# One attention and gate kernel: decay folded into V, token-block loads, row-tiled head pairs, one pipeline

## The chip, the core and the metric

The kernel runs on one core of a Trainium2 chip. Its time is the device time of one launch in microseconds (us), taken as the median of 3 runs. The core has TensorE (PE, with its weight loads PEld), VectorE (DVE), ScalarE (ACT), GpSimd (POOL) and SyncE (SP), which here issues most DMAs. Each engine runs its own instruction list in order and waits on semaphores for the others.

## The reference

Inputs are q, k, v of 8 batches, 8 heads, 576 positions, 64 numbers each, a selection signal s of 8 x 8 x 576, and three weights. In the reference's terms:

```
cum    = cumsum(max(s, 0))                       # per head, over positions
scores = q @ k.T / 8 + min(-(cum_q - cum_k), 0)  # causal: later keys are masked
attn   = softmax(scores) ;  x = attn @ v         # heads side by side: x is 576 x 512
gate   = sigmoid(sum over 5 taps of conv_w[t] * x shifted by 4 - t)
out    = (gate * (x @ w_val)) @ w_out            # 8 x 576 x 512, float32
```

The decay is a difference of running sums, so exp(-(cum_q - cum_k)) is a factor of the query times a factor of the key, and the query's factor cancels when a row is divided by its sum.

## The kernel before, in words

The tokens of a batch are cut in key blocks of 128, 128, 128, 128 and 64 (`kbs`, `kbo`). A set-up part computes the running sums with TensorE (`cumT`, lines 72 to 86) and loads the weights.

**Attention**, one batch after another (line 114 on): blocks of q, k and v come in as float32; TensorE transposes q and k in float32, two heads at a time (line 135), and ScalarE and VectorE copy each head to `QT` and `KT` (lines 142, 144). Row 64 of these holds the query's running sum and ones, so that a score matmul with 65 rows adds the query's decay (line 159); the key's decay is the bias of the exp (line 162). VectorE multiplies each diagonal block by a triangle (166). The products with V (line 175) carry a column of ones for the row sums; VectorE and ScalarE divide (180 to 184), TensorE transposes the result (187), and a copy puts it in `xT`.

**Gate**, after the last batch, for four groups of channels and eight batches (line 196 on): ScalarE multiplies by each tap (202, 206), VectorE adds (209), ScalarE takes the sigmoid (210), TensorE computes x @ w_val (214), VectorE multiplies (217). **Output**, last: TensorE (226), a copy on ScalarE (229), a store (230).

What runs when is set twice: the lists that the engines run come out of a scheduler that interleaves the program's operations by its own estimate of when they are ready, and the tile pools set how many copies of a tile exist (`ps_s`, `ps_t`, `ps_a`: two PSUM tiles each). All loads of q, k, v and all stores are issued by SyncE; the small loads of `cwT` (line 99) and of the decay rows (119) by ScalarE.

Of the kernel before, what the change touches and what calls it, by code (L numbers as in the profile page):

```python
# [8 lines left out]
FP32 = mybir.dt.float32  # L9
BF16 = mybir.dt.bfloat16  # L10
AF = mybir.ActivationFunctionType
ALU = mybir.AluOpType


@with_exitstack
def kernel(
# [11 lines left out]
    nc = tc.nc  # L28
    B, H, S, D = 8, 8, 576, 64
    DM = 512  # L30
    NKB = 5
    kbs = [128, 128, 128, 128, 64]
    kbo = [0, 128, 256, 384, 512]
    NT = B * S

    const_p = ctx.enter_context(tc.tile_pool(name="const", bufs=1))
    cum_p = ctx.enter_context(tc.tile_pool(name="cum", bufs=1))
    qk_in_p = ctx.enter_context(tc.tile_pool(name="qkin", bufs=3))
    qkt_p = ctx.enter_context(tc.tile_pool(name="qkt", bufs=2))
    v_p = ctx.enter_context(tc.tile_pool(name="v", bufs=2))  # L40
    attn_p = ctx.enter_context(tc.tile_pool(name="attn", bufs=2))
    x_p = ctx.enter_context(tc.tile_pool(name="x", bufs=1))
    moe_p = ctx.enter_context(tc.tile_pool(name="moe", bufs=1))
    glu_p = ctx.enter_context(tc.tile_pool(name="glu", bufs=1))
    gate_p = ctx.enter_context(tc.tile_pool(name="gate", bufs=2))
    oout_p = ctx.enter_context(tc.tile_pool(name="oout", bufs=3))
    ps_s = ctx.enter_context(tc.tile_pool(name="ps_s", bufs=2, space=bass.MemoryType.PSUM))
    ps_t = ctx.enter_context(tc.tile_pool(name="ps_t", bufs=2, space=bass.MemoryType.PSUM))
    ps_a = ctx.enter_context(tc.tile_pool(name="ps_a", bufs=2, space=bass.MemoryType.PSUM))

    ident = const_p.tile([128, 128], BF16)
    make_identity(nc, ident)
    identf = const_p.tile([128, 128], FP32)
    make_identity(nc, identf)
    triu_b = const_p.tile([128, 128], BF16)
    make_upper_triangular(nc, triu_b, 1.0, diag=True)
    triu_f = const_p.tile([128, 128], FP32)
    make_upper_triangular(nc, triu_f, 1.0, diag=True)
    ones_t = const_p.tile([128, 128], FP32)
    nc.gpsimd.memset(ones_t, 1.0)  # L60

    sp = cum_p.tile([64, S], FP32)
    nc.sync.dma_start(out=sp, in_=s.rearrange("b h s -> (b h) s"))
    nc.scalar.activation(out=sp, in_=sp, func=AF.Relu)
    cumT = [cum_p.tile([kbs[i], 64], FP32, name=f"cumT{i}") for i in range(NKB)]
    cumnat = cum_p.tile([64, S], FP32)
    cumneg8 = cum_p.tile([64, S], BF16)
    spT = cum_p.tile([128, NKB * 64], FP32)
    for i in range(NKB):
        n = kbs[i]  # L70
        pt = ps_t.tile([n, 64], FP32, name="tp")
        nc.tensor.transpose(pt, sp[:, kbo[i]:kbo[i] + n], identf[0:64, 0:64])
        nc.vector.tensor_copy(spT[0:n, i * 64:(i + 1) * 64], pt)
    for i in range(NKB):
        n = kbs[i]
        pc = ps_t.tile([n, 64], FP32, name="tp")
        for ip in range(i):
            nc.tensor.matmul(pc, ones_t[0:kbs[ip], 0:n], spT[0:kbs[ip], ip * 64:(ip + 1) * 64],
                             start=(ip == 0), stop=False)
        nc.tensor.matmul(pc, triu_f[0:n, 0:n], spT[0:n, i * 64:(i + 1) * 64],  # L80
                         start=(i == 0), stop=True)
        nc.vector.tensor_copy(cumT[i], pc)
        pn = ps_t.tile([64, n], FP32, name="tp")
        nc.tensor.transpose(pn, cumT[i], identf[0:n, 0:n])
        nc.scalar.copy(cumnat[:, kbo[i]:kbo[i] + n], pn)
    nc.scalar.activation(out=cumneg8, in_=cumnat, func=AF.Copy, scale=-8.0)

    wv = moe_p.tile([128, 4 * DM], BF16)
    wo = moe_p.tile([128, 4 * DM], BF16)
    for c in range(4):  # L90
        wtmp = qk_in_p.tile([128, 2 * DM], FP32, name="wtmp")
        nc.sync.dma_start(out=wtmp[:, 0:DM], in_=moe_w_val[c * 128:(c + 1) * 128, :])
        nc.sync.dma_start(out=wtmp[:, DM:2 * DM], in_=moe_w_out[c * 128:(c + 1) * 128, :])
        nc.gpsimd.tensor_copy(wv[:, c * DM:(c + 1) * DM], wtmp[:, 0:DM])
        nc.vector.tensor_copy(wo[:, c * DM:(c + 1) * DM], wtmp[:, DM:2 * DM])
    cwT = moe_p.tile([128, 4 * 5], FP32)
    for c in range(4):
        for kk in range(5):
            nc.scalar.dma_start(out=cwT[:, c * 5 + kk:c * 5 + kk + 1],
                                in_=moe_conv_w[kk:kk + 1, c * 128:(c + 1) * 128].rearrange("a p -> p a"))  # L100

    xT_all = [x_p.tile([128, NT], BF16, name=f"xT{c}") for c in range(4)]

    copy_engines = [nc.scalar, nc.vector]

    QT_sets = [[const_p.tile([65, S], BF16, name=f"QT{p}_{h}") for h in range(H)] for p in range(2)]
    KT_sets = [[const_p.tile([65, S], BF16, name=f"KT{p}_{h}") for h in range(H)] for p in range(2)]
    Vp_sets = [const_p.tile([128, H * NKB * 65], BF16, name=f"Vp{p}") for p in range(2)]
    for p in range(2):
        for h in range(H):  # L110
            nc.gpsimd.memset(KT_sets[p][h][64:65, :], 1.0)
        nc.gpsimd.memset(Vp_sets[p], 1.0)

    for b in range(B):
        QT = QT_sets[b % 2]
        KT = KT_sets[b % 2]
        Vp = Vp_sets[b % 2]
        for h in range(H):
            nc.scalar.dma_start(out=QT[h][64:65, :], in_=cumneg8[b * 8 + h:b * 8 + h + 1, :])  # L119
        eng_i = 0  # L120
        for i in range(NKB):
            n = kbs[i]
            vstage = qk_in_p.tile([128, 512], FP32, name="vstage")
            nc.sync.dma_start(out=vstage[0:n, :].rearrange("s (h d) -> s h d", h=8),
                              in_=v[b, :, kbo[i]:kbo[i] + n, :].rearrange("h s d -> s h d"))
            nc.gpsimd.tensor_copy(  # L126
                Vp.rearrange("p (h k) -> p h k", h=8)[0:n, :, i * 65:i * 65 + 64],
                vstage[0:n, :].rearrange("s (h d) -> s h d", h=8))
            for src, dstlist in ((q, QT), (k, KT)):
                stg = qk_in_p.tile([128, 512], FP32, name="qkstage")  # L130
                nc.sync.dma_start(out=stg[0:n, :].rearrange("s (h d) -> s h d", h=8),
                                  in_=src[b, :, kbo[i]:kbo[i] + n, :].rearrange("h s d -> s h d"))
                for c in range(4):
                    pt = ps_t.tile([128, n], FP32, name="tp")
                    nc.tensor.transpose(pt, stg[0:n, c * 128:(c + 1) * 128], identf[0:n, 0:n])  # L135
                    for h2 in range(2):
                        eng = copy_engines[eng_i % 2]
                        eng_i += 1
                        dst = dstlist[2 * c + h2][0:64, kbo[i]:kbo[i] + n]
                        srcp = pt[h2 * 64:h2 * 64 + 64, :]  # L140
                        if eng is nc.scalar:
                            eng.copy(dst, srcp)  # L142
                        else:
                            eng.tensor_copy(dst, srcp)  # L144

        for hp in range(4):
            attnT = [[attn_p.tile([kbs[i], S - kbo[i]], BF16, name=f"attnT{hh}_{i}")
                      for i in range(NKB)] for hh in range(2)]
            for hh in range(2):
                h = 2 * hp + hh  # L150
                bh = b * 8 + h
                for i in range(NKB):
                    n = kbs[i]
                    w = S - kbo[i]
                    qc0 = 0
                    while qc0 < w:
# [104 lines left out]
```

## Time and profile before

| | us |
|---|---|
| median of 3 runs (range) | 605.12 (604.73 to 605.56) |
| span of the profiled execution, first to last instruction | 603.7 |
| PE / DVE / ACT / POOL busy in it | 441.9 / 343.4 / 440.7 / 42.2 |

The profiled execution's time is known as its span; the 1.4 us between span and median lie around it. Busy times are sums over the whole span. Matmuls are pipelined, so that the durations of neighbours overlap and a busy PE is not PE at its peak. The granted clock is given as a share of 2.4 GHz; 0.50 is the other level, 1.2 GHz. L12 is line 12 of the kernel.

### The profile page before, as it was taken

How to read it: one execution, taken by the hardware profiler on the slowest of the kernel's cores; microseconds unless marked ns; L12 is line 12 of the kernel's file. 1: busy time of each engine (PE TensorE's matmuls, PEld its weight loads, DVE VectorE, ACT ScalarE, POOL GpSimd, SP SyncE). 2: the span in 40 equal slices, each digit the busy share in tenths (PEclk: the TensorE clock that was granted, in tenths of full speed). 3: DMA queues.
4: the chain of work that ended last, by engine and by line, in shares of the span. 5: the costliest groups of instructions: out<-in, count | busy, mean ns of one | idle time of the engine just before them, and what ended most of it. 6: DMA issues, size and time to landing. Idle time of an engine off the chain costs nothing.

```text
span 603.7 us, 8107 instructions
## 1 busy us (share of the span) xinstructions
PE 441.9 (73%) x2280; PEld 225.7 (37%) x2280; DVE 343.4 (57%) x1406; ACT 440.7 (73%) x1189; POOL 42.2 (7%) x75
## 2 busy tenths in 40 slices
PE   2558976986986897898898798888344544454987
PEld 2334543553543454444445444344111211121332
DVE  1245655565665565565566466555788888887000
ACT  1147868876886886786777687686999999998455
POOL 5701010001001001001000100000000000000000
PEclk9999999999999999999999999999755555555899
DMA  7354435115314413512522411100000000000566
GB/s 194 78 129 108 97 85 118 35 37 117 69 36 96 106 35 71 131 36 52 122 47 54 97 35 36 35 2 2 0 0 1 1 0 1 0 1 0 179 223 226
DMA packets 123964, 40.60 MB, mean 67 GB/s; under 512 B 118224, under 2 KB 118224, under 8 KB 123920
## 3 DMA queue, kind: packets, MB, share of 16 engines
q1 hardware_dynamic: 118992, 40.00, 26.9%
q10 hardware_dynamic: 4928, 0.09, 0.5%
q8 instruction: 18, 0.29, 0.2%
q14 instruction: 26, 0.21, 0.1%
HBM read 30.57 MB, written 9.44 MB: 66 GB/s over the span
## 4 chain that ended last, share of the span: by engine, by line
PE 42%; ACT 31%; DVE 14%; DMA 5%; issue 4%; ACTq 3%; SPq 0%; DVEq 0%
PE pss L159 13%; PE tp L135 11%; ACT tmp L206 11%; PE psa L175 10%; ACT attnT L162 9%; DVE gp L209 8%; ACT gp L210 3%; PE tpb L187 3%; DMA out_dram<-ot 3%; ACTq L119 2%; PE pss L226 2%; ACT KT L142 2%; DVE KT L144 2%; ACT QT L142 2%; DVE QT L144 1%
## 5 line engine op out<-in xcount | busy, mean ns | idle before, releaser
L162 ACT ACTIVATE attnT<-pss,cumT 128x512 bf16<-128x512 f32 (+5 forms) x384 | 175.2, 481 | 34.0 <-PE pss L159 28.2
L159 PE MATMUL pss<-QT,KT 65*128 65x512 bf16 (+5 forms) x384 | 136.9, 408 | 18.6 <-ACT attnT L162 8.4
L135 PE MATMUL tp<-identf,qkstage 128*128 128x128 f32 (+1 forms) x320 | 122.6, 434 | 37.9 <-DVE QT L144 18.1
L214 PE MATMUL pss<-xT,wv 128*128 128x512 bf16 (+1 forms) x256 | 64.5, 422 | 73.6 <-DVE glu L217 73.5
L175 PE MATMUL psa<-Vp,attnT 128*128 128x65 bf16 (+2 forms) x960 | 111.4, 249 | 4.0 <-DVE attnT L166 3.3
L209 DVE TENSOR_TENSOR gp<-gp,tmp 128x572 f32<-128x572 f32 (+3 forms) x128 | 91.9, 753 | 23.3 <-ACT tmp L206 21.7
L206 ACT ACTIVATE tmp<-xT,cwT 128x575 f32<-128x575 bf16 (+3 forms) x128 | 92.7, 764 | 6.3 <-DVE gp L209 6.0
L135 PEld LDWEIGHTS tp<-identf,qkstage 128*128 128x128 f32 (+1 forms) x320 | 57.6, 187 | 106.1 <-DVE KT L144 41.1
L175 PEld LDWEIGHTS <-attnT 128*128 128x128 bf16 (+2 forms) x960 | 81.5, 136 | 39.5 <-DVE attnT L166 18.0
L166 DVE TENSOR_TENSOR attnT<-attnT,triu_b 128x128 bf16<-128x128 bf16 (+1 forms) x320 | 64.7, 211 | 44.7 <-ACT attnT L162 42.1
L214 PEld LDWEIGHTS <-wv 128*128 128x128 bf16 x256 | 26.9, 134 | 110.3 <-issue 109.0
L144 DVE CAST QT<-tp 64x128 bf16<-64x128 f32 (+1 forms) x160 | 42.7, 278 | 29.0 <-ACT QT L142 25.6
L159 PEld LDWEIGHTS <-KT 65*128 65x128 bf16 (+1 forms) x384 | 47.0, 135 | 32.1 <-issue 19.3
L184 ACT ACTIVATE xp<-psa,rec 128x64 bf16<-128x64 f32 (+1 forms) x160 | 49.0, 311 | 10.8 <-DVE xp L183 3.7
L180 DVE RECIPROCAL rec<-psa 128x1 f32<-128x1 f32 (+1 forms) x160 | 26.4, 165 | 52.4 <-PE psa L175 51.4
L144 DVE CAST KT<-tp 64x128 bf16<-64x128 f32 (+1 forms) x160 | 41.6, 278 | 25.4 <-ACT KT L142 22.7
L142 ACT CAST KT<-tp 64x128 bf16<-64x128 f32 (+1 forms) x160 | 35.8, 247 | 24.6 <-PE tp L135 24.5
L142 ACT CAST QT<-tp 64x128 bf16<-64x128 f32 (+1 forms) x160 | 36.1, 245 | 21.7 <-PE tp L135 16.4
L187 PE MATMUL tpb<-ident,xp 128*128 128x128 bf16 (+1 forms) x160 | 45.2, 283 | 8.8 <-ACT xp L184 8.3
L183 DVE TENSOR_SCALAR xp<-psa,rec 128x64 bf16<-128x64 f32 (+1 forms) x160 | 44.7, 280 | 1.1
L126 POOL CAST Vp<-vstage 128x512 bf16<-128x512 f32 (+1 forms) x40 | 24.3, 626 | 288.4 <-PE psa L175 184.1
L226 PE MATMUL pss<-wo,glu 128*128 128x512 bf16 (+1 forms) x160 | 38.8, 392 | 2.7 <-ACT ot L229 1.7
(42 smaller groups left out, 242.1 us busy)
## 6 DMA issues: line engine op xcount, KB each, us to landing
vstage<-in_v_dram SPq DMA_DIRECT2D x32, 256.0 KB, 3.8
qkstage<-in_q_dram SPq DMA_DIRECT2D x32, 256.0 KB, 3.0
qkstage<-in_k_dram SPq DMA_DIRECT2D x32, 256.0 KB, 3.0
out_dram<-ot SPq DMA_DIRECT2D x32, 256.0 KB, 2.0
wtmp<-in_moe_w_val_dram SPq DMA_DIRECT2D x4, 256.0 KB, 3.5
wtmp<-in_moe_w_out_dram SPq DMA_DIRECT2D x4, 256.0 KB, 3.8
QT<-cumneg ACTq DMA_DIRECT2D x64, 1.1 KB, 2.4
vstage<-in_v_dram SPq DMA_DIRECT2D x8, 128.0 KB, 3.3
```

The lines of the kernel that those rows point to most:

```text
L135: nc.tensor.transpose(pt, stg[0:n, c * 128:(c + 1) * 128], identf[0:n, 0:n])
L142: eng.copy(dst, srcp)
L144: eng.tensor_copy(dst, srcp)
L159: nc.tensor.matmul(pss, KT[h][:, kbo[i]:kbo[i] + n], QT[h][:, kbo[i] + qc0:kbo[i] + qc0 + qcw], start=True, stop=True)
L162: nc.scalar.activation(out=attnT[hh][i][:, qc0:qc0 + qcw], in_=pss, func=AF.Exp, scale=0.125, bias=cumT[i][:, bh:bh + 1])
L166: nc.vector.tensor_tensor(attnT[hh][i][:, 0:n], attnT[hh][i][:, 0:n], triu_b[0:n, 0:n], ALU.mult)
L175: nc.tensor.matmul(psa[:, hh * 65:hh * 65 + 65], attnT[hh][i][:, co:co + nq], Vp[0:kbs[i], h * 325 + i * 65:h * 325 + (i + 1) * 65], start ...
L187: nc.tensor.transpose(ptx, xp, ident[0:nq, 0:nq])
L206: nc.scalar.activation(out=tmp[:, sh:S], in_=xc[:, o:o + S - sh], func=AF.Copy, scale=cwT[:, c * 5 + kk:c * 5 + kk + 1])
L209: nc.vector.tensor_tensor(gp[:, sh:S], gp[:, sh:S], tmp[:, sh:S], ALU.add)
L214: nc.tensor.matmul(psv, wv[:, dc * DM + c * 128:dc * DM + (c + 1) * 128], xT_all[dc][:, o + tok0:o + tok0 + tw], start=(dc == 0), stop=(dc ...
L226: nc.tensor.matmul(pso, glu[c][:, o:o + nq], wo[:, c * DM:(c + 1) * DM], start=(c == 0), stop=(c == 3))
```

## The change

The program is written anew as `main_path`, with the old method kept, nearly as it was, as `general_path`.

- **Decay.** VectorE computes the running sum with one scan, subtracts half of its last value, TensorE transposes it and ScalarE takes the exp: `w`, one factor per key and head. V and its column of ones are multiplied by `w` on GpSimd. The scores have 64 rows, the exp has no bias tensor.
- **Loads.** q and k of a token block come in for all heads, GpSimd casts them to bf16, five bf16 transposes of a head pair fill one PSUM tile, and one VectorE copy of 576 columns moves it.
- **Head pairs.** The two heads of a pair lie on rows 0 to 63 and 64 to 127 of `QT` and `KT`; their score matmuls go to two PSUM banks, and one exp covers 2 x 512 columns. The last key block's scores of a whole batch form one tile (`scores4`).
- **Gate.** sigmoid(z) is written as (1 + tanh(z/2))/2, with the half put into `wo`; VectorE does each of the four taps as one multiply and add.
- **One loop.** Step n does the scores of pair n, the V products of n-1, transposes for the next batch, the transpose and taps of pair n-2, and gate values and outputs of earlier ones.
- **Guard.** At the end every row sum's reciprocal is tested against 1e-34 and 3e31; all engines read the result and branch past `general_path`, which would otherwise run.

Of the diff, the new loop and what it calls (`general_path` and the small parts are left out):

```diff
+    nc.vector.tensor_tensor_scan(cum, sp, sp, 0.0, ALU.add, ALU.max)
+    nc.vector.tensor_scalar(chalf, cum[:, S - 1:S], 0.5, None, ALU.mult)
+    nc.vector.tensor_scalar(cum, cum, chalf, None, ALU.subtract)
...
+        nc.tensor.transpose(pt, cum[:, kbo[i]:kbo[i] + n], identf[0:64, 0:64])
+        nc.scalar.activation(out=w[0:n, i, :], in_=pt, func=AF.Exp)
...
+    def load(b):
...
+                nc.gpsimd.tensor_copy(dst[0:n, i, :], st[0:n, :])
...
+            nc.gpsimd.tensor_tensor(Vp[0:n, i, :, 0:64], st[0:n, :].rearrange("s (h d) -> s h d", h=8),
+                                    wb.unsqueeze(2).to_broadcast([n, 8, 64]), ALU.mult)
+            nc.gpsimd.tensor_copy(Vp[0:n, i, :, 64:65], wb.unsqueeze(2))
...
+    def qk_transpose(b, p, which):
...
+        pt = ps_m.tile([128, S], BF16, name="m")
...
+            nc.tensor.transpose(pt[:, kbo[i]:kbo[i] + n], src[0:n, i, p * 128:(p + 1) * 128],
+                                ident[0:n, 0:n])
+        nc.vector.tensor_copy(dst[:, p, :], pt)
...
+    STEPS = [
+        [(0, 0, 128, 0), (1, 128, 128, 128), (2, 256, 128, 256), (3, 384, 128, 384)],
+        [(0, 128, 448, 0), (3, 512, 64, 448)],
+        [(1, 256, 320, 0), (2, 384, 192, 320)],
+    ]
...
+        for (kb, q0, nq, c0) in STEPS[step]:
+            for hh in range(2):
+                r = slice(64 * hh, 64 * hh + 64)
+                nc.tensor.matmul(ps[:, hh, c0:c0 + nq], st["KT"][r, p, kbo[kb]:kbo[kb] + 128],
+                                 st["QT"][r, p, q0:q0 + nq], start=True, stop=True)
+        nc.scalar.activation(out=Pt[:, :, step * 512:(step + 1) * 512], in_=ps, func=AF.Exp, scale=0.125)
+        if step == 0:
+            dg = Pt[:, :, 0:512].rearrange("k h (g q) -> k h g q", g=4)
+            nc.vector.tensor_tensor(dg, dg, tri.unsqueeze(1).unsqueeze(1).to_broadcast([128, 2, 4, 128]),
+                                    ALU.mult)
...
+        for kk in range(4):
+            nc.vector.scalar_tensor_tensor(gp, xc[:, kk:kk + S], cwT[:, c * 5 + kk:c * 5 + kk + 1], gp,
+                                           ALU.mult, ALU.add)
...
+        nc.scalar.activation(out=th, in_=gp, func=AF.Tanh, scale=0.5)
...
+    for n in range(NS + 9):
...
+        if 0 <= n - 1 < NS:
+            b1, p1 = divmod(n - 1, 4)
+            fill += [lambda: av(b1, p1, 0), lambda: av(b1, p1, 1)]
+        if b + 1 < B:
+            fill += [lambda: qk_transpose(b + 1, p, 0), lambda: qk_transpose(b + 1, p, 1)]
+        if 0 <= n - 2 < NS:
+            b2, p2 = divmod(n - 2, 4)
+            fill += [lambda: (x_transpose(b2, p2), conv(b2, p2))]
...
+    good = nc.values_load(okcnt[0:1, 0:1], min_val=0, max_val=128)
+    with tc.If(good < 128):
+        with ExitStack() as c2:
+            general_path(c2, tc, *args)
```

The scheduler mixes these steps. Three places follow; a row is line, operation, tile written <- tiles read, shape written, and x is a count in a row. First, ScalarE at the start, before the change: the taps' small loads stand around the first operations on the running sum.

```order
L99 DMA cwT_208<-in_moe_conv_w_dram 128x1 x6
L64 ACT_TABLE_LOAD
L64 ACTIVATE sp_119<-sp_119 64x576
L99 DMA cwT_208<-in_moe_conv_w_dram 128x1 x10
L85 COPY cumnat_127<-tp_148 64x128
L99 DMA cwT_208<-in_moe_conv_w_dram 128x1 x2
L85 COPY cumnat_127<-tp_155 64x128
```

ScalarE at the start, after the change (w is the key weight, wv the value matrix, P the exps of a pair):

```order
L420 DMA cwT_229<-in_moe_conv_w_dram 128x1 x16
L253 ACT_TABLE_LOAD
L253 ACTIVATE w_127<-m_128 128x64
L253 ACTIVATE w_127<-m_131 128x64
L420 DMA cwT_229<-in_moe_conv_w_dram 128x1
L253 ACTIVATE w_127<-m_134 128x64
L253 ACTIVATE w_127<-m_137 128x64
L420 DMA cwT_229<-in_moe_conv_w_dram 128x1
L253 ACTIVATE w_127<-m_140 64x64
L416 ACTIVATE wv_203<-qkst_205 128x512
L416 ACTIVATE wv_203<-qkst_208 128x512
L305 ACTIVATE P4_370<-ps_361 64x512
```

Sixteen of the twenty small loads now stand ahead of all exps, where six stood ahead of the first operation. Second, TensorE in the middle of attention, before the change: V products of the last, 64-column query block, then scores of the next head.

```order
L175 MATMUL psa_3846<-Vp0_265,attnT1_3_3756 128x65
L175 LDWEIGHTS attnT0_0_3748
L175 MATMUL psa_3864<-Vp0_265,attnT0_0_3748 64x65
L175 LDWEIGHTS attnT0_4_3752
...
L159 MATMUL pss_3905<-QT0_6_239,KT0_6_255 128x320
L159 LDWEIGHTS KT0_6_255
L159 MATMUL pss_3909<-QT0_6_239,KT0_6_255 128x192
L187 LDWEIGHTS xp_3858
L187 MATMUL tpb_3861<-ident_97,xp_3858 128x128
```

TensorE in the middle of the loop, after the change: a transpose (kb, 128 rows), scores of two heads (KT, 64 rows), V products with the small last key block (P4, 64 rows) and the large ones (P, 128 rows):

```order
L292 MATMUL m_2243<-ident_104,kb_2118 128x128
L327 LDWEIGHTS KT_1664
L327 MATMUL ps_2489<-QT_1663,KT_1664 128x320
...
L327 MATMUL ps_2489<-QT_1663,KT_1664 128x192
L349 LDWEIGHTS P4_2181
L349 MATMUL psB_146<-Vp_1612,P4_2181 64x65
L349 LDWEIGHTS P_2198
L349 MATMUL psB_146<-Vp_1612,P_2198 64x65
...
L292 LDWEIGHTS qb_2117
L292 MATMUL m_2230<-ident_104,qb_2117 128x128
```

Scores of 64 rows now stand between 128-row transposes and V products, where they had 65 rows of the whole array. Third, VectorE in attention, before the change: divisions, triangle products and copies of single heads.

```order
L180 RECIPROCAL rec_3128<-psa_3117 64x1
L181 RECIPROCAL rec_3128<-psa_3117 64x1
L166 TENSOR_TENSOR attnT0_1_3138<-attnT0_1_3138,triu_b_107 128x128
L183 TENSOR_SCALAR xp_3131<-psa_3117,rec_3128 64x64
L144 CAST KT0_1_250<-tp_3343 64x128
L193 COPY xT2_231<-tpb_3114 128x128
```

VectorE in the loop, after the change (gp: a gate tap; glu: the gate product; m: a tile of the two-buffer PSUM pool):

```order
L332 TENSOR_TENSOR P_2198<-P_2198,tri_114 128x2x512
L378 SCALAR_TENSOR_TENSOR gp_1850<-xT_1481,cwT_229,gp_1850 128x576
L355 RECIPROCAL recs_143<-psB_146 128x4
...
L356 TENSOR_TENSOR xn_1800<-psB_146,recs_143 128x2x128
...
L294 COPY QT_1663<-m_1968 128x576
...
L294 COPY KT_1664<-m_1975 128x576
L370 COPY xT_1988<-m_1990 128x576
L394 SCALAR_TENSOR_TENSOR glu_2005<-th_1496,m_2006 128x288
L332 TENSOR_TENSOR P_2283<-P_2283,tri_114 128x2x512
```

The four taps of a gate tile (one of them shown) stand between the divisions and the copies that empty the PSUM pool.

## Rows read from the trace of the kernel before

**Rows 1.** Page, part 1: busy us of each engine, share of the span, instructions.

```profile
PE 441.9 (73%) x2280; PEld 225.7 (37%) x2280; DVE 343.4 (57%) x1406; ACT 440.7 (73%) x1189; POOL 42.2 (7%) x75
```

**Rows 2.** Busy time by stretch; columns as the heading says.

```profile
core 0: us, PE busy (x) PEld busy (x) DVE busy (x) ACT busy (x) POOL busy (x), PEclk, DMA share, GB/s
30.00:60.00 30.00, 22.06 (x98) 11.65 (x98) 14.64 (x70) 18.02 (x67) 3.71 (x6) 1.00 0.54 119
250.00:300.00 50.00, 43.57 (x240) 22.88 (x239) 29.44 (x161) 36.26 (x125) 2.98 (x5) 1.00 0.37 82
440.00:490.00 50.00, 24.82 (x96) 10.29 (x96) 41.24 (x69) 46.51 (x69) 0.00 (x0) 0.50 0.00 0
560.00:580.00 20.00, 19.74 (x82) 7.90 (x81) 0.00 (x0) 11.69 (x20) 0.00 (x0) 0.94 0.61 216
```

**Rows 3.** Page, part 4: the chain that ended last, by engine.

```profile
PE 42%; ACT 31%; DVE 14%; DMA 5%; issue 4%; ACTq 3%; SPq 0%; DVEq 0%
```

**Rows 4.** Timeline of PE near 254 us: start us, us, what, count.

```profile
252.25 0.54 PE L175 MATMUL psa<-Vp,attnT 128*128 128x65 bf16 x6
...
253.89 1.52 PE L175 MATMUL psa<-Vp,attnT 128*128 128x65 bf16 x14
...
255.85 0.26 PE L175 MATMUL psa<-Vp,attnT 128*128 128x65 bf16 x1
```

**Rows 5.** PE by form: count, busy us, mean ns, idle before.

```profile
L214 PE MATMUL pss<-xT,wv 128*128 128x512 bf16 x128 | 58.0, 603 | 73.6 <-DVE glu L217 73.5
L187 PE MATMUL tpb<-ident,xp 128*128 128x128 bf16 x128 | 37.9, 296 | 4.6 <-ACT xp L184 4.4
L226 PE MATMUL pss<-wo,glu 128*128 128x512 bf16 x128 | 31.2, 395 | 1.0 <-DVE glu L217 0.6 <-ACT ot L229 0.4
```

**Rows 6.** DVE by form, the same columns.

```profile
L166 DVE TENSOR_TENSOR attnT<-attnT,triu_b 128x128 bf16<-128x128 bf16 x256 | 54.0, 219 | 34.3 <-ACT attnT L162 32.0
...
L209 DVE TENSOR_TENSOR gp<-gp,tmp 128x575 f32<-128x575 f32 x32 | 24.3, 758 | 10.2 <-ACT tmp L206 10.1
...
L217 DVE TENSOR_TENSOR glu<-pss,gp 128x512 bf16<-128x512 f32 x32 | 22.1, 692 | 5.6 <-PE pss L214 2.1 <-ACT gp L210 1.2
L180 DVE RECIPROCAL rec<-psa 128x1 f32<-128x1 f32 x128 | 21.3, 166 | 30.0 <-PE psa L175 29.0
...
L193 DVE COPY xT<-tpb 128x128 bf16<-128x128 bf16 x64 | 14.4, 224 | 11.7 <-PE tpb L187 10.6
L166 DVE TENSOR_TENSOR attnT<-attnT,triu_b 64x64 bf16<-64x64 bf16 x64 | 11.4, 178 | 10.3 <-ACT attnT L162 10.1
...
L217 DVE TENSOR_TENSOR glu<-pss,gp 128x64 bf16<-128x64 f32 x32 | 6.9, 214 | 0.0
...
L193 DVE COPY xT<-tpb 128x64 bf16<-128x64 bf16 x16 | 3.1, 191 | 6.3 <-PE tpb L187 6.3
```

**Rows 7.** Timeline of DVE near 260 us.

```profile
260.38 0.35 DVE L166 TENSOR_TENSOR attnT<-attnT,triu_b 128x128 bf16<-128x128 bf16 x2
```

**Rows 8.** ACT by form.

```profile
L162 ACT ACTIVATE attnT<-pss,cumT 128x512 bf16<-128x512 f32 x64 | 44.0, 687 | 5.4 <-PE pss L159 4.1
L162 ACT ACTIVATE attnT<-pss,cumT 128x448 bf16<-128x448 f32 x64 | 40.6, 635 | 6.0 <-PE pss L159 2.4
...
L202 ACT ACTIVATE gp<-xT,cwT 128x576 f32<-128x576 bf16 x32 | 24.4, 764 | 1.1 <-DVE glu L217 0.8 <-issue 0.2
```

**Rows 9.** POOL's cast by form; a VectorE cast at the start, ns min/median/max.

```profile
L126 POOL CAST Vp<-vstage 128x512 bf16<-128x512 f32 x32 | 19.1, 620 | 264.1 <-PE psa L175 184.1 <-PE tpb L187 44.9 <-DMA vstage<-in_v_dram 25.9
...
L95 DVE CAST wo<-wtmp x4: 427/600/877, 5.8 to 15.9; 128x512 bf16<-128x512 f32 x4
```

**Rows 10.** Timeline of ACT at the start: its DMA issues.

```profile
0.75 3.49 ACTq L99 DMA_DIRECT2D cwT<-in_moe_conv_w_dram  x6
...
5.99 6.57 ACTq L99 DMA_DIRECT2D cwT<-in_moe_conv_w_dram  x10
```

**Rows 11.** DMA issues: count, KB each, median us to landing.

```profile
qkstage<-in_q_dram SPq DMA_DIRECT2D x32, 256.0 KB, 3.0
```

More of the change, by code (lines that the diff above doesn't have):

```diff
@@ L28 @@
     nc = tc.nc
[L29 to L107, printed above, removed]
@@ L220 @@
-    for b in range(B):
-        for qb in range(NKB):
-            nq = kbs[qb]
-            o = b * S + kbo[qb]
-            pso = ps_s.tile([nq, DM], FP32, name="pss")
-            for c in range(4):
-                nc.tensor.matmul(pso, glu[c][:, o:o + nq], wo[:, c * DM:(c + 1) * DM],
-                                 start=(c == 0), stop=(c == 3))
-            ot = oout_p.tile([nq, DM], FP32)
-            nc.scalar.copy(ot, pso)
-            nc.sync.dma_start(out=out[b, kbo[qb]:kbo[qb] + nq, :], in_=ot)
+    flag_p = ctx.enter_context(tc.tile_pool(name="flag", bufs=1))
@@ L234 @@
+    okcnt = flag_p.tile([1, 1], I32, name="okcnt")
+    args = (q, k, v, s, moe_w_val, moe_conv_w, moe_w_out, out)
+    with ExitStack() as c1:
+        main_path(c1, tc, *args, okcnt)
+    good = nc.values_load(okcnt[0:1, 0:1], min_val=0, max_val=128)
+    with tc.If(good < 128):
+        with ExitStack() as c2:
+            general_path(c2, tc, *args)
 _INS = ['q', 'k', 'v', 's', 'moe_w_val', 'moe_conv_w', 'moe_w_out']
```

483 lines of the change are left out of this document (375 added, 108 removed).

## The prediction

> **What bounds the kernel now.** I read the page's totals first, then the table by stages, then the chain, then the forms of each engine. No engine is full: TensorE is busy 441.9 of 603.7 us [rows 1], but that adds up two unlike stages [rows 2]. In attention (250 to 300 us) TensorE is busy 43.6 of 50, ScalarE 36.3, VectorE 29.4, at granted clock 1.00: many small instructions that wait for each other. In the gate stage (440 to 490) ScalarE is busy 46.5 of 50 and VectorE 41.2 while TensorE waits at clock 0.50, its 1.2 GHz level. The output stage is TensorE alone. The chain agrees: TensorE 42%, ScalarE 31%, VectorE 14% [rows 3]. So the old time is attention (about 390 us with the start), then gate (165), then output (45), one behind the other. The new kernel lays the three over one another, so its time is set by the fullest engine's own sum, plus a start, a tail and waits. I work out each engine's sum.
>
> **TensorE.** The new order holds 2432 matmuls of the loop: 960 for attention times V, 480 transposes (now bf16), 512 scores, 64 small scores, 256 gate values (288 columns), 160 outputs (512 columns). Price of a small one: six in a row take 0.54 us where a lone one takes 0.26, so five steps in about 0.28 to 0.29: 58 ns a step [rows 4]. Small ones are 960 + 480 + 256 + 64 + 64 = 1824, so 106 us. Price of a wide one: 512 columns take 31.2/128 = 0.244 us at near the full clock [rows 5], 0.477 ns a column: 64 scores each of 448, 320 and 192 columns 29.4 us, 256 x 0.137 = 35.1, 160 x 0.244 = 39.0. Streams: 210 us.
>
> On top comes the change of shape. The fourteen V products in a row [rows 4] change rows or columns of the array four times: thirteen steps in 1.52 - 0.26 = 1.26 us, nine of them at 58 ns, leaves 0.185 each for the four, 0.127 more than a step. The new order changes between 64 and 128 rows or columns 569 times (counted in the order), because the 64-row score pairs now stand between 128-row work, as the TensorE piece of the order shows: at most 72 us. The Trainium skill, "TensorEngine Tiling (Array Packing)", section Tiling Modes, states both sides: tiles of 64 rows run in parallel, up to twice as fast, but changing the tiling mode drains the engine. The trace agrees with the drain [rows 4]; no run here shows two row tiles side by side. By the rule the scores would take half, by the rows alone nothing is saved.
>
> Bounds: if two row tiles overlap fully, half of the scores' 48 us goes (-24) and if the changes hide, 72 goes too: 186. If each step between the row tiles 0 to 63 and 64 to 127 also costs a change (512 x 0.127), +65: 347. A transpose alone lasts 0.296 us [rows 5]; I count 58 ns, since a duration holds the latency that six in a row share. I take 210 + 55 = 265 us, three quarters of the changes, because some fall where TensorE waits anyway.
>
> **VectorE.** Gate taps 128 x 0.758 = 97 us; gate product of 288 columns, between 214 and 692 ns for 64 and 512: 453 ns x 64 = 29; reciprocals 64 x 0.17 = 11; normalise, 384 and 256 columns on the same line, 32 x (0.555 + 0.419) = 31; 96 copies of 576 bf16 columns, extrapolated from 191 and 224 ns for 64 and 128: 0.455, 44 us; causal mask of 1024 columns, from 178 and 219: 0.79, 32 times, 25; small masks 4 [rows 6]. Sum 241. Where two stand back to back they take less than two durations (0.35 for two of 0.219 [rows 7]), so 210 is as near. The mask now has a repeated operand that no row shows: at the slope of the f32 product (1.07 ns a column) it is 1.15 us, +11; no reason shows a gain.
>
> **ScalarE and GpSimd.** Exp of 512 columns 687, of 448 635 ns: 0.81 ns a column, so 1024 columns 1.10 us, x 96 = 106 [rows 8]. Gate start and tanh 64 x at most 0.764 = 49, output copies 40 and weights 8 at no more than 0.69, 33, small exps 6: 194 us, under both others. GpSimd: 80 casts x 0.62 = 50 [rows 9], 40 products with the weight, which no row shows: between a cast (0.62) and two (1.24), 25 to 50, I take 0.93; 40 tiny copies 5: some 92 us, 11.5 a batch against 33 a batch of TensorE, so hidden. What it can spoil is VectorE: the same cast there took 427 ns and 877 beside GpSimd's work [rows 9]. If that held for the two-input products all through, about +50 on VectorE: 290, and it would be the bound. The Trainium skill, "GPSIMD Engine Reference", section Specifications, says that the two share SBUF interfaces when VectorE has two SBUF inputs; these rows agree for a cast.
>
> **Start, loads, tail.** ScalarE issues sixteen of the twenty tiny weight loads before the exps that make the key weights (ScalarE piece of the order). In the old run those sixteen take 3.49 + 6.57 us [rows 10], so the weights are ready at about 14. GpSimd stands behind them with its first V product; after it come 7 casts, 5 products and tiny copies, 10.5 us, then a transpose and a copy: pairs start at 25.5. Batch 1 follows 23 DMAs: 9.2 MB with its own; 119 GB/s at 0.54 share [rows 2] is 220 GB/s, 42 us plus one landing of 3.0 [rows 11]: 45. Batch 0's four pairs, each 16 scores (1.4), 30 V products with five changes (2.4) and some waits, cover 25.5 to about 44, so this costs 0 to 5, taken as 1. Behind the last exp come mask, V, normalise, transpose, copy (5), eight gate taps of two pairs (6), tanh and product (1), five outputs (5), copy and store (3), the guard (2, bounded by 0 and 10, since no row has one: every engine reads the count before its branch, and on SyncE the read stands ahead of the last store, which waits for it): 22, of which 10 is TensorE work already counted: +12.
>
> **Waits.** The attention stage leaves its busiest engine idle 13%, the gate stage 7% [rows 2]. I take 10% of 265: 26.
>
> **Sum.** 25.5 + 1 + 265 + 12 + 26 = 329.5 us of span. The old span is 603.7 against a median of 605.12, 1.4 more: 331 us.
>
> **Rivals.** (a) Overlap: row tiles run side by side and changes hide; then VectorE bounds: 25.5 + 230 + 10 behind it + 6% waits (14) + 1.4 = 281. For it: VectorE's sum is nearly as large. Against: the drain in the fourteen. (b) Two buffers: each pair sends 6.25 tiles (two Q/K, one x, two gate values, 1.25 outputs) through the two buffers of one PSUM pool. A tile is held for its fill (about 0.6), VectorE's queue and the copy (0.455). The VectorE piece of the order has up to four gate taps ahead of a copy, 3 us; with 2.4 us of queue it is 3.4 x 6.25 / 2 = 10.7 us a pair, 341 in all, and 380 with start and tail. It decides once the hold is over 2.9 us. (c) Clock: if the waits let the granted clock fall to 0.50 as in the gate stage, wide matmuls go from 0.244 to 0.453 us [rows 5], 103 to 192 us; over the whole loop +89, 420 and over. Against: in attention it stays at 1.00, and the new loop is denser. (d) Slower than before: the guard. After the main path the reciprocals of all row sums must lie between 1e-34 and 3e31, else the whole general path runs behind it, some 600 us more as today: 930 us. It decides on a single row. From the inputs, the decay over 576 keys is 102 to 130 per head, so halved exponents reach 65 and the reciprocals 9e-30 to 1.3e28, inside by three orders of magnitude or more. That also answers whether the fold does its work.
>
> **How the numbers follow.** Forecast 331: 0.54, own range 305 to 360. (a) 0.20, (b) 0.15, (c) 0.09, (d) 0.02. Range 288 to 390: it takes in most of (a) and (b), VectorE's +50 (25.5 + 290 + 10 + 26 + 1.4 = 353) and a third of the +65, and leaves out (c), (d) and the ends, some 2 in 10. Faster by over 0.2% (about what a measurement can tell from no change) holds in all but (d): 0.97, the same 0.01, slower 0.02.
>
> **What would show it.** TensorE busy nearly throughout at clock 1.00, first large exp at 25 to 28 us, no gap at 45; matmul steps of 58 ns with breaks at each 64-row piece; VectorE taps at 0.76 us. Wrong: score pairs starting a few ns apart (a); TensorE waiting mostly for copies of the transposes (b); granted clock near 0.5 in the loop (c); instructions of the general path (d).

## The result and the profile after

The changed kernel takes 349.76 us (median of 4 runs, 348.80 to 355.78) where the kernel before took 605.34 in the same series: ratio 0.577, interval [0.576, 0.578]. The profiled execution took 348.80 with a span of 347.2 us. The forecast was 331 with its own range of 305 to 360: the direction and the main mechanism held, and about 18 us are to be explained. Medians below are over all runs of a kernel; ratios and their intervals leave disturbed runs out, and no ratio is given where too few are left.

Busy time of each engine after the change, part 1 of the page, and from its part 2 TensorE's busy tenths and granted clock in 40 slices of 8.7 us; these answer to [rows 1]:

```profile
PE 270.9 (78%) x2439; PEld 161.2 (46%) x2439; DVE 244.8 (70%) x466; ACT 168.7 (49%) x222; POOL 125.0 (36%) x179
...
PE   0236984878688798879997989889887998993990
...
PEclk9999999999999789955996798658995799696797
```

Attention, gate and output now lie over one another, and TensorE and VectorE are both nearly full at once. The clock row is new: it reads full for about the first 115 us and then moves between its two levels (a mean of 0.5 is the 1.2 GHz level). For the first 107 us that reading is wrong, as the part on TensorE below shows; in the next table this touches the clock of the first six rows. The chain that ended last, by engine, answers to [rows 3]: VectorE has taken ScalarE's place beside TensorE.

```profile
PE 41%; DVE 34%; ACT 10%; DMA 6%; issue 3%; POOL 3%; ACTq 1%; DVEq 0%; POOLq 0%
```

The table by stretch, cut at the exps, is the view that finds the missing time: to the first exp (29.8); to where exps stop (48.97); to the next exp (64.28); three pieces of the second and third batch; the steady loop to the last exp; and the tail.

```profile
core 0: us, PE busy (x) PEld busy (x) DVE busy (x) ACT busy (x) POOL busy (x), PEclk, DMA share, GB/s
0.00:29.80 29.80, 9.56 (x61) 5.40 (x62) 6.62 (x14) 3.49 (x9) 14.63 (x40) 1.00 0.95 186
29.80:48.97 19.17, 15.68 (x158) 9.36 (x157) 7.36 (x17) 15.16 (x19) 5.54 (x7) 1.00 0.94 186
48.97:64.28 15.31, 9.97 (x79) 6.29 (x80) 5.04 (x13) 0.78 (x2) 10.21 (x19) 1.00 0.83 142
64.28:74.00 9.72, 7.51 (x75) 4.72 (x75) 9.47 (x16) 7.53 (x9) 8.87 (x5) 1.00 1.15 172
74.00:90.98 16.98, 11.85 (x126) 8.33 (x123) 6.83 (x19) 6.39 (x7) 5.57 (x14) 1.00 0.29 61
90.98:107.60 16.62, 15.10 (x114) 8.44 (x114) 15.23 (x24) 8.03 (x9) 13.44 (x16) 1.00 1.33 210
107.60:299.60 192.00, 168.67 (x1614) 100.80 (x1615) 163.08 (x306) 110.73 (x142) 66.78 (x84) 0.81 0.48 101
299.60:347.20 47.60, 32.58 (x223) 17.85 (x220) 31.12 (x63) 16.61 (x28) 0.00 (x0) 0.82 0.22 77
```

Length less PE busy gives TensorE's idle time: 20.2 us before the first exp, then 3.5, 5.3, 2.2, 5.1, 1.5 up to 107.6, 23.3 in the steady loop (12% of it) and 15.0 in the tail: 76 us, and with 270.9 busy that is the span. The forecast had 64.5 idle and 265 busy. In the steady loop TensorE (88%) and VectorE (85%) are both close to full; from 48.97 to 64.28 and from 74 to 91 no engine is.

**The first gap.** The timeline of ScalarE there, and of GpSimd (start us, us, what, count, idle before and its releaser):

```profile
47.95 1.02 ACT L329 ACTIVATE P<-ps 128x1024 bf16<-128x1024 f32 x1 [1.11 <-PE ps L327]
62.73 0.78 ACT L376 ACTIVATE gp<-xT,cwT 128x576 f32<-128x576 bf16 x1 [13.76 <-DVE xT L370]
```

```profile
43.17 0.61 POOL L274 CAST qb<-qkst 128x512 bf16<-128x512 f32 x1
51.46 0.72 POOL L281 CAST Vp<-w 128x8 bf16<-128x8 f32 x5 [7.68 <-PE psB L349]
52.10 0.60 POOL L274 CAST kb<-qkst 128x512 bf16<-128x512 f32 x1
```

GpSimd stands still for 7.68 us although its next loads have landed (behind the wait nine casts and products follow without one for a DMA): in its queue the tiny copies of batch 2 (line 281, the key weight beside V) have been put ahead of casts of batch 1, and they write into the V buffer that batch 0's products still read. The pool has two. The same wait returns at 75 us; the waits of the whole span show it as 20.9 us in four pieces:

```profile
POOL Vp L281 <- PE psB L349: 20.9, 4, 11.4
```

**VectorE.** By form (count, busy us, mean ns, idle before), answering to [rows 6]; under it the gate taps', the mask's and GpSimd's V products' own durations, minimum/median/maximum in ns, and when the first and last started:

```profile
L378 DVE SCALAR_TENSOR_TENSOR gp<-xT,cwT,gp 128x576 f32<-128x576 bf16 x128 | 118.0, 926 | 5.3 <-ACT gp L376 5.0
L394 DVE SCALAR_TENSOR_TENSOR glu<-th,m 128x288 bf16<-128x288 f32 x64 | 28.7, 450 | 10.9 <-PE m L392 10.5
L332 DVE TENSOR_TENSOR P<-P,tri 128x1024 bf16<-128x1024 bf16 x32 | 27.6, 861 | 2.0 <-ACT P L329 1.9
L356 DVE TENSOR_TENSOR xn<-psA,recs 128x384 bf16<-128x384 f32 x32 | 17.6, 551 | 0.3
L294 DVE COPY QT<-m 128x576 bf16<-128x576 bf16 x32 | 14.5, 455 | 31.1 <-PE m L292 31.0
...
L356 DVE TENSOR_TENSOR xn<-psB,recs 128x256 bf16<-128x256 f32 x32 | 13.3, 417 | 0.3
```

```profile
L378 DVE SCALAR_TENSOR_TENSOR gp<-xT,cwT,gp x128: 773/814/1852, 64.5 to 330.1; 128x576 f32<-128x576 bf16 x128
L332 DVE TENSOR_TENSOR P<-P,tri x32: 645/684/2570, 31.8 to 305.3; 128x1024 bf16<-128x1024 bf16 x32
L279 POOL TENSOR_TENSOR Vp<-vst,w x40: 1036/1047/6272, 11.6 to 259.6; 128x512 bf16<-128x512 f32 x32, 64x512 bf16<-64x512 f32 x8
L394 DVE SCALAR_TENSOR_TENSOR glu<-th,m x64: 440/450/456, 101.1 to 334.4; 128x288 bf16<-128x288 f32 x64
```

A mean far above its median is the thing to see. Taps and mask, which read both tensors from SBUF, have maxima of 2 to 4 times the median, and so has GpSimd's product, up to 6.27 us; the gate product, which reads one from PSUM, never leaves 440 to 456 ns.

**The tail.** SyncE's timeline at the end; the three stores issue until 340.92, and the span ends 6.3 us later.

```profile
337.80 3.12 SPq L406 DMA_DIRECT2D out_dram<-ot  x3
```

### The profile page after: what moved, and what is told of

Read it like the earlier page. It is cut to its first block, busy times and chain, and to the rows that moved or that the text cites. A ratio compares the mean times of both kernels' runs of the same rounds, so it can differ in the third digit from the quotient of the medians.

```text
span 347.2 us, 6219 instructions
## 1 busy us (share of the span) xinstructions
PE 270.9 (78%) x2439; PEld 161.2 (46%) x2439; DVE 244.8 (70%) x466; ACT 168.7 (49%) x222; POOL 125.0 (36%) x179
## 4 chain that ended last, share of the span: by engine, by line
PE 41%; DVE 34%; ACT 10%; DMA 6%; issue 3%; POOL 3%; ACTq 1%; DVEq 0%; POOLq 0%
DVE gp L378 21%; PE m L392 9%; PE psB L349 8%; PE m L292 7%; PE ps L327 6%; ACT P L329 6%; PE psA L349 4%; DVE P L332 4%; PE m L368 4%; DMA cwT<-in_moe_conv_w_dram 3%; DVE glu L394 3%; PE m L402 2%; DVE xn L356 2%; DVE QT L294 1%; ACT gp L376 1%
## 5 line engine op out<-in xcount | busy, mean ns | idle before, releaser
L378 DVE SCALAR_TENSOR_TENSOR gp<-xT,cwT,gp 128x576 f32<-128x576 bf16 x128 | 118.0, 926 | 5.3 <-ACT gp L376 5.0
L329 ACT ACTIVATE P<-ps 128x1024 bf16<-128x1024 f32 x96 | 95.7, 1025 | 48.9 <-PE ps L327 48.6
L349 PEld LDWEIGHTS <-P 128*128 128x128 bf16 (+2 forms) x960 | 57.6, 118 | 37.2 <-issue 16.9
L327 PE MATMUL ps<-QT,KT 64*128 64x128 bf16 (+4 forms) x512 | 62.0, 297 | 12.8 <-ACT P L329 11.6
L279 POOL TENSOR_TENSOR Vp<-vst,w 128x512 bf16<-128x512 f32 (+1 forms) x40 | 52.9, 1322 | 28.0 <-DMA vst<-in_v_dram 21.3
L392 PE MATMUL m<-xT,wv 128*128 128x288 bf16 x256 | 51.0, 347 | 8.9 <-DVE xT L370 6.2
L349 PE MATMUL psB<-Vp,P 128*128 128x65 bf16 (+2 forms) x576 | 53.2, 226 | 5.3 <-DVE xn L356 3.9
L381 ACT ACTIVATE th<-gp 128x576 f32<-128x576 f32 x32 | 21.9, 684 | 48.4 <-DVE glu L394 48.2
L402 PE MATMUL m<-wo,glu 128*128 128x512 bf16 (+1 forms) x160 | 39.7, 389 | 0.2
L274 POOL CAST qb<-qkst 128x512 bf16<-128x512 f32 (+1 forms) x40 | 31.1, 779 | 21.6 <-DMA qkst<-in_q_dram 20.9
L274 POOL CAST kb<-qkst 128x512 bf16<-128x512 f32 (+1 forms) x40 | 30.7, 769 | 16.1 <-DMA qkst<-in_k_dram 16.1
L376 ACT ACTIVATE gp<-xT,cwT 128x576 f32<-128x576 bf16 x32 | 24.9, 778 | 21.3 <-DVE xT L370 20.9
L292 PE MATMUL m<-ident,qb 128*128 128x128 bf16 (+1 forms) x160 | 24.2, 258 | 12.8 <-POOL qb L274 10.2
```

The source lines that it names most:

```text
L274: nc.gpsimd.tensor_copy(dst[0:n, i, :], st[0:n, :])
L279: nc.gpsimd.tensor_tensor(Vp[0:n, i, :, 0:64], st[0:n, :].rearrange("s (h d) -> s h d", h=8), wb.unsqueeze(2).to_broadcast([n, 8, 64]), AL ...
L292: nc.tensor.transpose(pt[:, kbo[i]:kbo[i] + n], src[0:n, i, p * 128:(p + 1) * 128], ident[0:n, 0:n])
L327: nc.tensor.matmul(ps[:, hh, c0:c0 + nq], st["KT"][r, p, kbo[kb]:kbo[kb] + 128], st["QT"][r, p, q0:q0 + nq], start=True, stop=True)
L329: nc.scalar.activation(out=Pt[:, :, step * 512:(step + 1) * 512], in_=ps, func=AF.Exp, scale=0.125)
L349: nc.tensor.matmul(ps[0:nq, j, hh, :], lhsT, Vp[0:n, kb, 2 * p + hh, :], start=(kb == 0), stop=(kb == qb))
```

## The experiments

**Two causes, one change each.** Three buffers for V; and, apart from it, the casts of q and k on ScalarE:

```diff
-    v_p = P("v", 2)
+    v_p = P("v", 3)
```

> V tiles of three batches instead of two (v_p bufs 3). Theory A (starved loads): GpSimd sat 7.6 us (43.8 to 51.4) and 11.4 us (75.2 to 86.6) behind small copies into the V tile of the batch after next, which waits for the V products of the batch before; behind them stood the casts of q and k. With a third tile these waits go; of the 19 us some 8 to 14 come off the end: 336 to 342 us, and no stretch of 15 us without an exp near 50 to 64 us. Theory B (TensorE's own sum sets the time, the early gaps are only filled later): 347 to 351 us.

Measured: 340.71 us (336.86 to 341.91), ratio 0.563 [0.561, 0.565]: 9 us less, in theory A's range. GpSimd's timeline at the same place now has the casts of batch 1 first:

```profile
48.46 0.61 POOL L274 CAST kb<-qkst 128x512 bf16<-128x512 f32 x1 [0.31 <-DMA qkst<-in_k_dram]
50.16 1.04 POOL L279 TENSOR_TENSOR Vp<-vst,w 128x512 bf16<-128x512 f32 x1 [1.09 <-DMA vst<-in_v_dram]
...
57.13 0.72 POOL L281 CAST Vp<-w 128x8 bf16<-128x8 f32 x5
```

The second batch starts at 61.1 instead of 65.2 and the third at 101.0 instead of 107.6. GpSimd now waits for loads only there, so not all of the hole goes: exps still pause from 49.6 to 60.2.

```diff
-                nc.gpsimd.tensor_copy(dst[0:n, i, :], st[0:n, :])
+                nc.scalar.copy(dst[0:n, i, :], st[0:n, :])
```

> The 80 casts of q and k to bf16 on ScalarE instead of GpSimd; V tiles stay two. Theory A with contention: the gate taps, 0.926 us on average (0.81 with GpSimd idle, 1.05 beside it), fall to 0.83 to 0.86, VectorE's busy time from 245 to about 233; ScalarE goes from 169 to about 218 us busy; the casts no longer stand behind GpSimd's waits: 335 to 344 us. Theory B: taps get faster, but the time stays at 347 to 352; and if ScalarE's list delays the exps (casts that wait for loads in front of exps): 355 to 370.

Measured: 339.38 us (336.66 to 344.12), ratio 0.560 [0.556, 0.564]: theory A's time, though the taps, at 0.882 us, stay above its 0.83 to 0.86. Since this also lets the casts pass GpSimd's waiting copies (the second batch starts at 59.7), it does not tell the two causes apart; the later runs do.

**Row tiles.** The two heads of a pair written one after the other instead of in turn:

```diff
-        for (kb, q0, nq, c0) in STEPS[step]:
-            for hh in range(2):
+        for hh in range(2):
+            for (kb, q0, nq, c0) in STEPS[step]:
```

> Scores of one head after those of the other within a step (loop over heads outside), so that neighbours on TensorE mostly lie on the same 64 rows. Theory A: two row tiles run side by side now (starts 33 to 54 ns apart at the 1.2 GHz level, where 128 columns alone take 107), worth up to half of the scores' 48 us; serial scores cost 8 to 24 us where TensorE sets the pace: 356 to 372 us. Rival: the pairs gain nothing in time because the exps wait elsewhere: 348 to 352 us.

Measured: 354.46 us (351.92 to 360.73), ratio 0.583 [0.580, 0.587]: about 4 us by the ratios, between the two theories. It is not the price of the pairs, though, because the new order does not take the overlap away. In the changed kernel two scores of 448 columns, one of each head, take the time of one (0.56 us, and the next operation 0.48 us behind the start either way):

```profile
39.86 0.55 PE L327 MATMUL ps<-QT,KT 64*128 64x448 bf16 x1
44.83 0.56 PE L327 MATMUL ps<-QT,KT 64*128 64x448 bf16 x2
```

And the four scores of a step, two of 448 and two of 64 columns, take as long in the changed kernel (first line) as in this run (second):

```profile
35.59 0.61 PE L327 MATMUL ps<-QT,KT 64*128 64x448 bf16 x4
36.32 0.61 PE L327 MATMUL ps<-QT,KT 64*128 64x448 bf16 x4
```

By the starts in the traces the two wide scores of a pair begin within 6 ns of each other for 21 of the 32 pairs in the changed kernel, and within 14 ns for 17 of them here. The Trainium skill, "TensorEngine Tiling (Array Packing)", section Tiling Modes, has the tiles of 64 rows run in parallel; this trace agrees. What the overlap is worth in all no run here shows.

**The guard.** Left out, with the general path behind it:

> Without the guard (the test of the reciprocals, its read by all engines, the branch and the general path are left out; nothing else). Before the change the last store was issued 3.2 us before the end of the span, now 6.8 us, and 0.8 us later than its tile was ready: theory A gives 4.4 us less, 345 us. Rival: a program half as long also starts or loads faster, 340 us or less; or the tail hides it: 349.

Measured: 345.62 us (343.90 to 348.62), ratio 0.571 [0.567, 0.575]: about 4 us, theory A's 345, where the forecast had counted 2. The first exp comes no earlier (30.3 us), so the shorter program does not start faster. Its last stores issue until 341.72, and the span ends 2.8 us later instead of 6.3:

```profile
339.38 2.34 SPq L406 DMA_DIRECT2D out_dram<-ot  x3
```

**The gate's buffers.** Five instead of two, since tanh waits 48.2 us for them in the changed kernel:

```diff
-    gate_p = P("gate", 2)
+    gate_p = P("gate", 5)
```

> Five buffers instead of two for the gate's tiles, nothing else. In the changed kernel the tanh of ScalarE waits 13 times, 48.2 us in all, for the gate product to free its buffer, and exps stand behind it in the queue. Theory A (TensorE's own sum and the load gap set the time; these waits lie in ScalarE's idle half): 346 to 351 us, no clear change. Theory B (the waiting tanh holds up exps, and with them TensorE, whose scores wait 11.6 us for exps): 336 to 343 us, and the row of scores waiting for exps falls to under 5 us.

Measured: 347.67 us (341.97 to 352.61): theory A's range by the median, and the spread takes in B's end. The wait of tanh for the gate product is gone from the long rows, but the scores wait longer for exps, 18.0 us against 11.6: theory B's mechanism does not show.

**The overlay.** Gate and output behind all of attention:

```diff
-            fill += [lambda: (x_transpose(b2, p2), conv(b2, p2))]
+            fill += [lambda: x_transpose(b2, p2)]
...
+    for n in range(NS + 4):
+        if n < NS:
+            conv(*divmod(n, 4))
+        if n >= 4:
+            val(*divmod(n - 4, 4))   # and the outputs behind each fourth
```

> The one pipeline undone in part: gate and output are written behind the attention of all batches (the scheduler still draws the first four gate starts and two tanh forward); eight buffers for x. Theory A (the overlay is worth what the engines' sums say): attention takes TensorE's 190 us of my sum plus waits, the gate stage then VectorE's taps and products, 133 us, and a start of 30 and a tail of 10 to 15: 370 to 395 us. Theory B (what the overlay saves is lost to contention with GpSimd, to changes of the array's shape and to the clock at 1.2 GHz): 345 to 360 us; then the taps in the gate stage take 0.81 us, without GpSimd's work beside them.

Measured: 403.50 us (401.40 to 406.48), ratio 0.665 [0.662, 0.668]. Theory A's sign, and 8 us above its range: the one pipeline is worth 54 us. The table by stretch shows where the rest comes from:

```profile
100.00:150.00 50.00, 42.54 (x409) 26.60 (x407) 24.21 (x58) 21.40 (x23) 14.49 (x29) 0.50 0.57 88
150.00:200.00 50.00, 43.41 (x422) 26.54 (x424) 23.29 (x56) 20.78 (x22) 20.98 (x33) 0.57 0.88 142
200.00:250.00 50.00, 43.82 (x415) 26.78 (x411) 23.54 (x57) 18.30 (x19) 15.51 (x25) 0.53 0.36 67
...
300.00:350.00 50.00, 35.53 (x158) 16.43 (x157) 47.01 (x74) 25.43 (x40) 0.00 (x0) 0.80 0.20 74
```

Attention alone runs at 0.50 to 0.57 of the clock with VectorE half idle; the gate stage is VectorE's, its taps at 0.820 us on the mean over the run, GpSimd being silent there. The same matmuls are 305.1 us busy here and 270.9 in the one loop, so part of the 54 us is TensorE's slower pace.

**Together.** Three V buffers, five for the gate, six stages instead of four, casts on ScalarE:

> Three buffers for V, five for the gate's tiles, six stages for loads, and the casts of q and k on ScalarE. Theory A (the load gap and the contention are two terms; three V buffers removed the one for 9 us, the casts moved removed both for 10): 328 to 337 us, with no batch longer than 36 us after the second. Theory B (both earlier runs removed the same gap, and ScalarE, now with 200 us of work, delays the exps): 337 to 345 us.

Measured: 332.08 us (326.96 to 334.64); taps 0.866, and theory A's range, though two later batches take 36.6 and 37.0 us, over its 36. In place of the casts on an engine, casts in the DMA, from GpSimd's queue:

```diff
-                nc.sync.dma_start(out=st..., in_=src...)
-                nc.gpsimd.tensor_copy(dst[0:n, i, :], st[0:n, :])
+                nc.gpsimd.dma_start(out=dst..., in_=src...)
```

> As the combination, but q and k are turned to bf16 by the DMA itself, issued from GpSimd's queue: no cast on any engine. Theory A (contention and casts are what is left): the taps take at most 0.88 us, ScalarE stays at 169 us busy, 325 to 335 us. Theory B (issuing the transfers costs GpSimd time and these transfers are slower, so V and q, k come late): 345 to 375 us, with TensorE waiting for DMA instead of casts.

Measured: 333.96 us (332.37 to 335.96), ratio 0.550 [0.548, 0.553]; taps 0.865. GpSimd is as busy as before (126 us), but with issues of 0.85 to 0.90 us each, and VectorE is as free as in the combination. Theory B's mechanism is there too, though not its time: the first large exp comes at 39.2 us instead of 30.8, and TensorE waits 20 us in all for these loads.

**The start.** On the combination, the twenty tiny loads moved to SyncE, and the small scores behind the first pair's:

```diff
-            steps = [lambda: scores4(b)] + steps
+            steps = steps + [lambda: scores4(b)]
-            nc.scalar.dma_start(out=cwT[...
+            nc.sync.dma_start(out=cwT[...
```

> The combination with two edits at the start: the twenty tiny weight loads are issued from SyncE, behind the loads of batch 0, and the small scores of a batch stand behind its first pair's scores, so that the first exp does not wait for the transposes of all four pairs. Theory A (the start is a term of its own, 30 us where I forecast 25.5): the first exp at 25 to 27 us, 327 to 330 us in all. Theory B (the first exps only come earlier to wait for the loads of batch 1, which end no sooner): 330 to 334 us, the second batch still starting at about 61 us.

Measured: 336.40 us (329.21 to 339.81). The first exp comes at 25.2 us instead of 30.1, yet the second batch's first exp is at 61.7 as in the combination (61.6), ScalarE having waited between its casts for loads: theory B's mechanism. The times do not decide: the median is 2 us above B's range, and the fastest run lies in A's.

**Contention by itself.** The combination with only q's casts on ScalarE; then its buffers with all casts on GpSimd; then without the gate's five:

> As the combination, but only the casts of q are on ScalarE, those of k stay on GpSimd. Theory A (GpSimd's work beside VectorE costs time): the taps take 0.88 to 0.90 us between the combination's 0.866 and the changed kernel's 0.926, and the time is 2 to 6 us longer than the combination's 332. Theory B (with the load gap gone the contention is hidden beside TensorE): the same 330 to 333 us.

> Only the buffers of the combination: three for V, five for the gate's tiles, six stages for loads; all casts stay on GpSimd. Theory A (what the combination gains over three V buffers alone, 332 against 341 us, comes from taking casts off GpSimd, beside which VectorE is slow): 338 to 342 us, taps at 0.92 us. Theory B (it comes from buffers, so that loads and gates run further ahead; the contention is hidden beside TensorE): 330 to 335 us with the taps still at 0.92 us.

> As the run before, but the gate's tiles keep two buffers: three for V and six stages alone. If the gain of the combination is due to the stages (loads further ahead): 330 to 335 us. If it is due to the gate's buffers, or to the casts: 338 to 342 us, as with three V buffers alone.

Measured: 332.04 us (329.07 to 334.79), ratio 0.546 [0.542, 0.549]; 346.94 (339.76 to 351.92), ratio 0.562 [0.560, 0.565]; 343.55 (341.32 to 346.75), ratio 0.566 [0.562, 0.570]. The buffers alone give nothing over three for V (0.563); the third kernel, at 343.55 us, rules out the stages as the cause (330 to 335), and the second comes to 341 us by its ratio, in theory A's range, though not by its median. The first two kernels differ by forty casts alone, and by 0.017 of 606 us: 10 us, at least 6 by the ends of the intervals. That is theory A's side of the second expectation, with taps of 0.873 us on the mean in the first profile and 0.968 and 0.920 in the other two. Taking k's casts off as well brings nothing further by the medians (332.08), theory B's side of the first. The loop from 107 to 299 us, with all casts on GpSimd (the third kernel), with q's on ScalarE (the first), and of the combination (columns as above):

```profile
107.00:299.00 192.00, 168.12 (x1600) 100.94 (x1606) 163.04 (x309) 110.57 (x144) 64.08 (x78) 0.83 0.48 101
```

```profile
107.00:299.00 192.00, 168.36 (x1662) 101.84 (x1662) 161.96 (x320) 121.87 (x166) 46.19 (x59) 0.84 0.49 108
```

```profile
107.00:299.00 192.00, 166.89 (x1691) 103.61 (x1692) 163.94 (x327) 132.85 (x190) 28.84 (x40) 0.87 0.49 108
```

With the same busy time VectorE gets 320 and 327 instructions done instead of 309, and TensorE 1662 and 1691 instead of 1600, as GpSimd's work beside them falls from 64 us to 46 and 29. The clock is not what separates the first two rows (0.83 and 0.84); in the third it may have a share (0.87). Nor is it that q comes earlier: TensorE's matmuls wait longer for its casts on ScalarE (the first kernel) than on GpSimd (the third):

```profile
PE m L292 <- ACT qb L274: 9.9, 6, 2.8
```

```profile
PE m L292 <- POOL qb L274: 5.8, 3, 2.2
```

## Why the prediction was right, and where it was not

**TensorE, 265 forecast, 270.9 busy.** That the sum is so near is luck: errors of opposite sign met in it.

*The clock.* I read the old attention as full clock [rows 2]. The profile reads 1.00 there, and in the first 107 us of the changed kernel, but the traces hold no record of the clock before 422.5 and 106.7 us. TensorE's own pace says the lower level. Twelve V products of the changed kernel take as long at 75.8 us, where the profile reads 1.00, as at 187.5 (granted 0.50), and less at 236.9 (granted 1.00, on record):

```profile
75.83 0.84 PE L349 MATMUL psA<-Vp,P 128*128 128x65 bf16 x12
187.51 0.84 PE L349 MATMUL psA<-Vp,P 128*128 128x65 bf16 x12
236.85 0.54 PE L349 MATMUL psA<-Vp,P 128*128 128x65 bf16 x12
```

By its starts in the trace a small step is thus 54 ns at the lower level and 29 at the upper, and the 58 ns taken from [rows 4] are the lower level's; the wide matmuls I priced near the upper one (0.244 us for 512 columns; here 0.216 at the upper and 0.427 at the lower). The changed kernel is at the lower level for about 90 us by its clock rows from 107.6 on and, by its pace, for the first 107, over half of the span. So the full clock that I forecast did not come, and much of rival (c) did. "The new loop is denser" was no reason for the full clock, since the old attention did not have it either: there as in the staged run TensorE was 42.5 to 43.8 us of 50 busy at or near the lower level. What raises it in the one loop these runs do not settle.

*The row tiles and the changes of shape.* I took no overlap of row tiles; the wide pairs run in the time of one, the first half of rival (a). A change of shape between V products adds about 0.12 us to a step at the lower level and 0.095 at the upper (0.127 taken), and the trace has 570 of them (569 counted): that term held. How much each error is worth in all is not measured.

**VectorE, 241 by durations or 210 with overlaps forecast, 244.8.** Copies 0.455, gate product 0.450, normalise 0.551 and 0.417 came as worked out from [rows 6]. The taps did not: 0.926 for 0.758, 21 us. Of that 7 us is the operation (0.814 is its median) and the rest goes with GpSimd: in the tail, where GpSimd is silent, taps take 0.81 to 0.82. I had priced this contention at up to 50 us and put it into the range, not into the forecast; it came to about 20 us of VectorE's busy time, 14 on the taps and 6 on the mask above its median. The experiments make it 10 us of time for the casts of q. The Trainium skill, "GPSIMD Engine Reference", section Specifications, ties it to VectorE operations in a 2-port perf mode or with two SBUF inputs; the trace agrees for two inputs, with 0.65 to 2.57 us for the mask and 440 to 456 ns throughout for the product that reads PSUM. The cast of [rows 9] has one SBUF input, so it is no instance of that half, as I had read it.

**ScalarE 194 forecast, 168.7; GpSimd 92 forecast, 125.** Both stay under the bound. The V product takes 1.05 us by its median (0.93 taken), 1.32 on the mean.

**Start, 25.5 forecast, 29.8.** The weights came earlier than I said (the last ends at 12.8 for 14), the first exp later, since it is one of the small scores, which need the transposes of all four pairs. This seems to have cost nothing: the run that moved it to 25.2 started its second batch no sooner.

**The failed step: batch 1's loads, "costs 0 to 5, taken as 1".** I timed the transfers and not the queue behind them. Batch 1's casts stand on GpSimd behind copies for batch 2, which wait for batch 0's products to leave the V buffer. The gap of exps is 15.3 us, and 9 us of the time went with a third buffer. It is the largest single term missing from the sum. I had asked what stands behind a waiting instruction on ScalarE and SyncE, and on GpSimd only for its first V product; the rest of its queue I took as 92 us of work hidden beside 265. The sign "no gap at 45" failed with it, as did the taps at 0.76 us and the clock of 1.00.

**Tail, 22 us behind the last exp, net +12.** It is 47.6, since 23 gate taps, not eight, are left then; but TensorE works in 32.6 of it, so net it is 15.0, of which the guard has 4 where I took 2. The guard's test is done at 320.7 us, yet its count comes at 339.1, because the matmul that sums it stands on TensorE behind the last outputs; no run here moves it.

**Waits, 26.** In the steady loop TensorE idles 23.3 us beside 168.7 busy, 14%, for the 10% taken. Its five batches take 36.2 us each (small exps from 107.6 to 288.6), for 36.4 worked out (265 + 26, by 8).

**The rivals.** (a) came in part, by its overlap of row tiles. (b), two PSUM buffers, did not decide: five steady batches at 36 us are not its 43. (c) came for over half of the span. (d), the guard's general path, did not run.

**Sum of the misses,** in TensorE's idle time: the stretches from 29.8 to 107.6 17.6 us where 1 and two batches of waits (6.5) were counted, +10.1; steady loop with the last batch's waits 23.3 for 19.5, +3.8; tail +3.0; busy +5.9; start 20.2 for 25.5, -5.3, as I had counted TensorE's first transposes twice. Together +17.5 of the 17.7 us.

## What to carry to other kernels

When stages are laid over one another, sum the engines first, then walk every queue for an instruction of a later batch that waits for a buffer and has the next batch's work behind it; here a third buffer for V, one changed number, gave 9 us. Where VectorE is within a tenth of the bound, put simple casts on an engine that is half idle and does not slow it: here forty casts moved from GpSimd to ScalarE gave 10 us. The best kernels of this study, at 332 us, do both.

## What the hardware showed that was not expected

- The contention goes both ways: GpSimd's V product takes 1.04 us alone and up to 6.27, VectorE's taps 0.77 to 1.85, its mask 0.65 to 2.57 us.
- Two score matmuls of 448 columns on the two row tiles take the time of one, and writing the heads one after the other does not change that.
- A clock of 1.00 in the profile can mean that no record is there: before the first one the steps of the same matmuls are 54 ns, as at 0.50, where 1.00 on record has 29.
- The guard (test, count, read by every engine, branch) costs about 4 us, with nothing in the branch run; 3.5 us of it lie behind the last stores.
